# Seven half-size products for part of the first feed-forward matmul, with one set of keys and queries, in a sparse-attention and feed-forward kernel on one Trainium2 core

## The chip, the core and the metric

The kernel runs on one core of one Trainium2 chip. The core has five engines that run side by side and wait for each other through semaphores: TensorE (PE; its weight loads are listed as PEld), VectorE (DVE), ScalarE (ACT), GpSimd (POOL) and SyncE (SP). TensorE writes its results into PSUM, eight banks of 512 float32 per partition; VectorE and ScalarE read and write PSUM, GpSimd does not in this kernel. Each engine takes its instructions strictly in the order of its queue; transfers are issued from SP's queue and from GpSimd's. The metric is the device time of one execution, in microseconds (us). Three runs of the kernel before gave 212.04 us as their median, from 211.33 to 214.41.

## The reference

Four batches of eight heads, 768 positions, head size 64. Every query sees the keys fewer than 16 positions away, and one summary for each of 24 blocks of 32 keys (the maximum of the block's keys, with log 32 added to its score, and the mean of its values). The attention output of all heads, 3072 tokens by 512, goes through a feed-forward layer with a gelu in its sigmoid form:

```
mask_l = np.abs(pos[:, None] - pos[None, :]) < window          # window = 16
scores_s = scale * q @ k_sum.T + np.log(block)                 # k_sum: max over blocks of 32
a = softmax(concat([where(mask_l, scale * q @ k.T, -1e9), scores_s]))
x = a @ concat([v, v_sum])                                     # 3072 x 512 after joining the heads
h = x @ w_in                                                   # 512 x 2048
out = (h * sigmoid(1.702 * h)) @ w_out                         # 2048 x 512
```

Work on the chip is in 16-bit types with float32 accumulation.

## The kernel before

All work is written in one list of words, `ORDER`; each word calls one small function (the table `ops`, near the end, says which), and the list's order is the order of every engine's queue. A batch goes through these steps:

- **Loads and keys.** `lk`, `lq`, `lv` load keys, queries and values (GpSimd's queue, with a cast to bfloat16). Batch 1 is transposed on TensorE (`tk`, `tq`); batches 2 and 3 by transposing transfers on SP's queue (`xk` for keys, `xq` for queries). `xa` takes the block maxima of the keys for two pairs of heads (VectorE), `ka` copies the key halos, `kR` writes the maxima into the key tiles. `vm` sums the values by blocks on TensorE, `vb` finishes the sums, `sd` and `ha` copy block sums and value halos (SP). `gate` is a small copy on GpSimd that waits for such a copy, and so holds back the loads behind it.
- **Attention.** `s` scores, `e` exponential (ScalarE), `m` mask (VectorE), `v` weighted values, `nn` normalisation (VectorE), `t`/`c` or `d` the transposition of the result into `xT` (TensorE and a copy, or a transfer).
- **First feed-forward matmul (an "ff stage").** There are 16 tiles of 128 hidden units (nt), each for the left and the right half of the 768 tokens. The word `f.half.nt.k0123.bank` makes four matmuls of 384 columns, `g` the gelu of that half tile (ScalarE) into `gT`.
- **Second matmul (a "product stage").** Each batch is done in three steps t by Winograd's form of Strassen's scheme: seven products `p.t.1` to `p.t.7` of eight matmuls with 256 columns, where the plain form has eight. `gs` builds the four sums of gelu results it needs (VectorE, some on GpSimd), `ws` the four sums of the weights (once), `x` takes the products out of PSUM: products 1, 5 and 6 are copied to SBUF, 2, 3 and 7 are added to such a copy on VectorE, 4 is copied. `o` stores. The accumulators are `poA`, `poB`, `poC`.

While the products of one batch run, the attention of the next is put between them; so product stages carry scores, exponentials, masks and norms, and ff stages carry the loads, transposes and key maxima of the batch after. Batch 0 is started by a path of its own. In the text, ff 1 is the ff stage of batch 1, products 1 its product stage, and so on.

Two memory pools matter. Keys `kx`, queries `qT` and values `vw` exist twice; batches 0 and 2 use set 0, batches 1 and 3 set 1. Set 0 lies in the pool `even`. The function `seven_pool` closes that pool and can open another in its place; the list calls it as its last but two word (`P7.0`), where it opens nothing. The functions for seven products in the first matmul (`w_sum7`, `x_sum7`, `product7`, `taken7`, `gelu7`) are in the file, but the list calls none of them.

PSUM is six pools: banks 0 to 3 single, 4 and 5 double. `bank(42, ...)` and `bank(52, ...)` take a double bank, 40, 41, 50, 51 half of one. The ff tiles use 0 to 3.

Of the kernel before, what the change touches and what calls it, by code (L numbers as in the profile page):

```python
# [17 lines left out]
class _Ordered:  # L18


    def __init__(self, tc, eng):
        self._tc, self._eng = tc, eng

    def __getattr__(self, name):
        f = getattr(self._eng, name)

        def call(*a, **kw):
            r = f(*a, **kw)  # L28
            self._tc.keep_in_program_order(r)
            return r  # L30

        return call
# [11 lines left out]
f.0.2.k0123.1 s.0.1.3.42 e.1.3 f.0.1.k23 f.0.4.k0123.50 mf f.0.6.k0123.40 f.0.5.k0123.51 f.0.7.k0123.41 G f.0.3.k0123.0  # L44
g.0.2 g.0.0 g.0.1 g.0.4 g.0.6 g.0.3 lk.1.3 lq.1.0 g.0.7 g.0.5 lq.1.3 ck.1 m.1.0 m.1.2 ow.1 lk.1.4 lk.1.1 lk.1.2 lv.1.5.1
lk.1.5 lk.1.6 lq.1.2 lk.1.7 m.1.1 lq.1.1 lv.1.0.0 lq.1.4 lq.1.5 lq.1.7 lv.1.3.1 lq.1.6 lv.1.0.1 lv.1.2.0 lv.1.1.0 cv.1
lv.1.1.1 lv.1.4.0 lv.1.2.1 f.0.8.k0123.2 lv.1.4.1 late m.1.3 ws.0.0 g.0.8 f.0.9.k0123.3 f.0.11.k0123.0 g.0.9
f.0.10.k0123.1 v.0.1.0.40 v.0.1.1.41 lv.1.3.0 nn.1.0 g.0.11 g.0.10 v.0.1.2.50 f.0.13.k0123.3 f.0.12.k0123.2 t.1.0.42
v.0.1.3.51 nn.1.1 f.0.15.k0123.0 g.0.12 f.0.14.k0123.1 g.0.13 t.1.1.52 c.1.0.d c.1.1.d g.0.15 ws.0.1 g.0.14 f.1.8.k01.3
f.1.0.k01.2 f.1.8.k23 ha.1.3.0 f.1.9.k0123.0 f.1.0.k23 ws.1.1 g.1.8 g.1.9 f.1.1.k0123.1 ws.2.0 f.1.2.k0123.3 g.1.0  # L50
f.1.3.k0123.2 g.1.1 ws.1.0 gs.0.2.0 ha.1.2.0 f.1.10.k0123.1 g.1.3 gs.0.2.1 f.1.4.k0123.2 g.1.2 gs.2.2.2 g.1.10 lv.1.5.0
gs.0.2.3 f.1.11.k0123.1 g.1.4 f.1.12.k0123.3 g.1.11 f.1.13.k0123.0 ws.3.1 tk.0.52 g.1.13 gs.2.2.0 g.1.12 kc.0.a
f.1.6.k0123.2 gs.0.2.2 gs.2.2.1 f.1.15.k0123.0 f.1.5.k0123.1 ws.3.0 g.1.6 g.1.5 tk.1.52 kc.1.a tk.2.42 kh.0.1.d ws.2.1
f.1.14.k0123.3 f.1.7.k0123.1 tk.3.52 gs.2.2.3 kc.2.a xm.0.1 tq.0.42 gs.4.2.0 g.1.15 kc.3.d p.0.2.0 g.1.7 g.1.14 gs.6.1.0
p.0.1.2 qc.0.a xm.1.1 tq.1.52 ha.1.1.0 gs.4.2.2 lq.2.0 x.0.1.a gs.4.2.1 gs.6.1.2 lq.2.2 gs.6.1.1 gs.7.1.0 ha.1.0.0
qc.1.a gs.6.1.3 lv.2.0.0 tq.2.42 p.1.1.3 qc.2.a gs.7.1.1 gs.4.2.3 p.0.5.1 x.0.5.a p.0.6 tq.3.52 kr.0.1.d s.1.0.0.42
x.0.6.a x.0.2.a gs.7.1.2 X gs.7.1.3 kr.1.1.d x.1.1.d xm.3.1 kh.2.1.g p.1.2.0 e.0.0 p.0.3 p.0.7 lq.2.3 m.0.0 x.0.3.a
x.0.7.a kh.1.1.d qc.3.d s.1.1.0.42 e.1.0 p.1.6 xm.2.1 vm.1.42 o.0.0.0.0.2 s.1.0.1.52 lv.2.5.0 e.0.1 kr.2.1.g kh.3.1.d
p.0.4 vb sd.1.1.0 x.0.4.a gate.1 s.1.1.1.52 e.1.1 lv.2.3.0 p.1.5.1 kr.3.1.d x.1.5.d x.1.2.a m.1.0 x.1.6.a s.1.0.2.52
sd.1.0.0 p.2.1.2 m.0.1 x.2.1.a p.1.3 s.1.0.3.42 o.0.0.1.0.2 p.1.7 lv.2.1.1 e.0.2 m.1.1 lk.2.0 e.0.3 s.1.1.2.52 lk.2.2  # L60
lv.2.2.0 x.1.7.a x.1.3.a lv.2.2.1 lk.2.3 p.2.6 e.1.2 lv.2.5.1 s.1.1.3.42 m.0.2 p.1.4 v.1.0.0.50 e.1.3 v.1.0.1.51 lk.2.1
m.0.3 m.1.3 lk.2.4 v.1.1.0.40 v.1.1.1.41 x.2.6.a p.2.5.1 G lk.2.5 nn.0.0 nn.1.0 x.2.5.a lk.2.7 p.2.7 o.0.1.0.0.2
# [20 lines left out]
f.0.0.k23 lk.3.6 g.0.1 g.0.9 g.0.8 f.1.1.k0123.0 f.1.8.k0123.1 g.0.0 f.1.9.k0123.3 g.1.1 g.1.9 g.1.8 f.1.0.k0123.2
f.0.10.k0123.0 g.0.10 gate.2 g.1.0 gs.0.2.2 xk.1.1.0 f.1.2.k0123.1 gs.0.2.0.d gs.0.2.1 xk.1.0.1 f.1.10.k0123.3 g.1.2
o.1.1.1.0.2 g.1.10 lq.3.6 f.0.2.k0123.2 gs.0.2.3 lv.3.5.1 f.1.3.k0123.1 vm.3.52 g.1.3 xk.1.1.1 g.0.2 xk.1.0.0
o.1.2.1.0.2 f.0.13.k0123.0 f.0.3.k0123.2 f.1.11.k0123.3 f.0.12.k0123.1 g.0.3 g.0.13 g.1.11 xa.0.1 f.0.4.k0123.2 xq.1.1
f.1.12.k0123.3 lq.3.1 f.0.11.k0123.0 g.0.4 gs.2.2.2.g g.0.12 f.1.5.k0123.1 g.0.11 lq.3.2 vb xa.1.1 xq.1.0 f.0.5.k0123.2
# [12 lines left out]
f.1.13.k0123.3 g.1.2 f.1.3.k0123.1 g.0.10 f.0.3.k0123.2 g.1.13 f.1.10.k0123.3 g.0.3 f.0.11.k0123.0 f.0.4.k0123.2 g.1.3  # L100
# [13 lines left out]
def kernel(  # L114
# [849 lines left out]
```

## Time and profile before

| | before |
|---|---|
| median of three runs | 212.04 us |
| the profiled execution | 211.7 us, of it 210.0 us span from first to last instruction |
| granted TensorE clock | 0.996 |
| busy: TensorE / VectorE / ScalarE / GpSimd | 200.4 / 130.8 / 114.3 / 109.1 us |
| ff 1, ff 2, ff 3 | 77.21 to 99.32, 123.10 to 144.63, 167.10 to 187.90 us |
| products 0, 1, 2, 3 | 51.6 to 77.2, 99.3 to 123.1, 144.6 to 167.1, 187.9 to 206.4 us |

The profile is one execution, read by several views: the groups of instructions (line, engine, operation, tile written `<-` tiles read, shape, count | busy us and mean ns of one | idle time of the engine before them and what ended it); the timeline, which merges neighbours of one kind (start, length, engine, instruction, count, and in brackets the engine's idle time before); the chain that ended last; and the busy time in stretches. All lines stand under one source line, 28, since a helper issues every instruction, so the groups are told apart by their tiles: `ph` is the accumulator of the first matmul, `ps_s` of scores, `ps_av` of weighted values.

### The profile page before, as it was taken

The page shows a single profiled execution, that of the slowest core. Times are in us where ns is not written, and L with a number is a line of the kernel's source. Part 1 is how long each engine was busy: PE and PEld are TensorE (multiplying, and loading weights), DVE is VectorE, ACT ScalarE, POOL GpSimd, SP SyncE. Part 2 cuts the span into 40 slices and gives each one's busy share as a digit, 9 for nine tenths or more (in the row PEclk, how much of TensorE's full clock was granted, in tenths as well). Part 3 has the DMA queues.
Part 4 walks back from the last instruction along what each step waited for, and adds up shares of the span by engine and source line. Part 5 has one row for each costly group of instructions (what it writes and reads, how often), then busy time and mean ns, then how long its engine had stood idle before and what let it go on. Part 6 is the DMA issues. An engine that isn't in the chain of part 4 may idle for free.

```text
span 210.0 us, 5880 instructions
## 1 busy us (share of the span) xinstructions
PE 200.4 (95%) x2440; PEld 145.8 (69%) x2440; DVE 130.8 (62%) x311; ACT 114.3 (54%) x227; POOL 109.1 (52%) x157
## 2 busy tenths in 40 slices
PE   7998798999999999999999999999999999999993
PEld 5656554667887886556788865657888865668882
DVE  5577873798997871168997822694888500166342
ACT  2473885659666736676764336567670157671100
POOL 7999972399982998448949422431000000863000
PEclk9999999999999999999999999999999999999998
DMA  4999999999999999999999999939215920000214
GB/s 67 162 166 189 209 213 221 182 144 122 99 134 199 156 177 183 130 126 141 148 166 204 142 227 180 187 29 169 50 53 139 160 105 0 0 3 0 100 53 150
DMA packets 96458, 27.74 MB, mean 132 GB/s; under 512 B 85024, under 2 KB 93488, under 8 KB 96432
## 3 DMA queue, kind: packets, MB, share of 16 engines
q0 software_dynamic: 70800, 13.64, 82.7%
q1 hardware_dynamic: 25632, 13.74, 33.2%
q8 instruction: 19, 0.31, 0.6%
q14 instruction: 7, 0.06, 0.1%
HBM read 27.26 MB, written 6.29 MB: 160 GB/s over the span
## 4 chain that ended last, share of the span: by engine, by line
PE 79%; POOL 12%; DMA 5%; issue 1%; DVE 1%; SPq 0%; POOLq 0%; DVEq 0%
PE ph L28 36%; PE poA L28 19%; PE poB L28 10%; PE poC L28 5%; PE ps_s L28 3%; PE ps_av L28 3%; DMA vw<-vw 2%; POOL mk L28 2%; DMA out_dram<-osb 2%; POOL v0n L28 2%; POOL w_in_sb L28 2%; POOL kb L28 2%; POOL kx L28 2%; POOL qb L28 1%; PE ps_t L28 1%
## 5 line engine op out<-in xcount | busy, mean ns | idle before, releaser
L28 PE MATMUL ph<-xT,w_in_sb 128*128 128x384 f16 x512 | 86.1, 326 | 0.4 <-DVE osb L28 0.4
L28 ACT ACTIVATE gT<-ph 128x384 f16<-128x384 f32 x128 | 56.1, 495 | 30.6 <-PE ph L28 29.9
L28 PEld LDWEIGHTS <-w_in_sb 128*128 128x128 f16 x512 | 49.2, 98 | 32.4 <-issue 0.9
L28 PEld LDWEIGHTS <-gs 128*128 128x128 f16 x384 | 36.5, 98 | 4.6
L28 DVE TENSOR_TENSOR gs<-gT 128x768 f16<-128x768 f16 (+1 forms) x36 | 17.5, 498 | 29.1 <-ACT gT L28 29.0
L28 POOL TENSOR_TENSOR gs<-gs,gT 128x768 f16<-128x768 f16 (+1 forms) x6 | 8.8, 1461 | 41.8 <-PE ph L28 32.7
L28 POOL DMA_DIRECT2D kb<-in_k_dram x28 | 23.1, 842 | 13.7 <-DMA w_out_sb<-in_moe_w_out_dram 6.4
L28 ACT ACTIVATE a_sb<-ps_s 128x768 bf16<-128x768 f32 x32 | 24.8, 808 | 9.5 <-PE ps_s L28 9.3
L28 PEld LDWEIGHTS <-gT 128*128 128x128 f16 x288 | 27.3, 98 | 3.6
L28 POOL DMA_DIRECT2D vw<-in_v_dram x36 | 25.7, 752 | 5.0 <-DMA w_out_sb<-in_moe_w_out_dram 1.7
L28 PE MATMUL poA<-ws,gs 128*128 128x256 f16 x192 | 24.8, 273 | 0.0
L28 POOL DMA_DIRECT2D qb<-in_q_dram x28 | 23.8, 867 | 1.8 <-issue 0.9
L28 DVE TENSOR_TENSOR a_sb<-a_sb,mk 128x768 bf16<-128x768 bf16 x28 | 14.7, 550 | 3.0 <-ACT a_sb L28 2.2
L28 DVE TENSOR_TENSOR x<-ps_av,rc 128x768 f16<-128x768 f32 (+1 forms) x18 | 15.6, 869 | 0.6
L28 ACT ACTIVATE s<-poA 128x256 f32<-128x256 f32 x14 | 5.4, 382 | 19.3 <-PE poA L28 18.6
L28 PE MATMUL poB<-ws,gs 128*128 128x256 f16 x96 | 12.5, 273 | 0.0
L28 PE MATMUL poC<-w_out_sb,gT 128*128 128x256 f16 x96 | 12.5, 273 | 0.0
L28 PE MATMUL poA<-w_out_sb,gT 128*128 128x256 f16 x96 | 12.4, 273 | 0.0
L28 PE MATMUL poB<-w_out_sb,gs 128*128 128x256 f16 x96 | 12.4, 273 | 0.0
L28 PE MATMUL poA<-ws,gT 128*128 128x256 f16 x96 | 12.3, 273 | 0.0
L28 DVE TENSOR_REDUCE ka<-kx 128x48 bf16<-128x1536 bf16 x4 | 7.0, 1750 | 7.4 <-DMA kx<-kb 7.4
L28 ACT ACT_TABLE_LOAD x8 | 10.3, 1283 | 0.9 <-PEq L948 0.8
(102 smaller groups left out, 219.0 us busy)
## 6 DMA issues: line engine op xcount, KB each, us to landing
out_dram<-osb SPq DMA_DIRECT2D x23, 256.0 KB, 2.9
kb<-in_k_dram POOLq DMA_DIRECT2D x24, 96.0 KB, 6.0
qb<-in_q_dram POOLq DMA_DIRECT2D x24, 96.0 KB, 5.0
vw<-in_v_dram POOLq DMA_DIRECT2D x36, 64.0 KB, 5.1
w_out_sb<-in_moe_w_out_dram POOLq DMA_DIRECT2D x4, 512.0 KB, 14.8
w_in_sb<-in_moe_w_in_dram POOLq DMA_DIRECT2D x3, 512.0 KB, 11.3
vw<-vs SPq DMA_DIRECT2D x6, 198.0 KB, 3.9
kb<-in_k_dram POOLq DMA_DIRECT2D x4, 192.0 KB, 4.4
```

The source lines that it names most:

```text
L28: r = f(*a, **kw)
```

## The change

**The list.** In batches 1, 2 and 3 three, three and six of the eight pairs of ff tiles (j, j + 8) are made by seven products: pairs 2, 3, 4, again 2, 3, 4, and 2 to 7. The words `f` and `g` of these tiles go (48 half tiles), and for each pair come seven words `P.j.1` to `P.j.7` of two matmuls with 384 columns, four words `S` and three words `H`. Per batch four `U` build sums of `xT` (the token side), and eight words `W` in batches 0 to 2 build the sums of `w_in` for pairs 2 to 4 and 5 to 7, all on VectorE. The list after batch 0's first ff tiles is new throughout: batch 0's calls of the weighted values, the sums `ws` and `gs`, the loads, the transfers and the products stand in other places. GpSimd has as many `gs` words as before.

**A pair.** Products 1 and 5 open the two halves l and r of a double bank, "X". S1 copies l into a single bank "A" (ScalarE in batches 1 and 2, VectorE in batch 3), S5 copies r to SBUF as "h" (ScalarE). Product 2 is added to l; product 6 to A. S6 (VectorE) writes A + h into r; product 3 is added to r, product 7 to A. S7 (VectorE) adds A to h; product 4 is added to A. Then `H.j.0` makes the gelu of l and r at once (768 columns), `H.j.1` that of A, `H.j.2` that of h.

**One set of keys and queries.** `scores` reads set 1 for batches 1, 2 and 3, and `xk`, `xq` write it; values keep two sets. `P7.6.2`, called after batch 0's last scores, closes the pool with set 0 and opens the pool of the seven products in its place, for six pairs beginning at 2.

**Sums in place.** The third of the four `gs` sums is written over the right half of `gT` of tiles 0 to 7, of which nothing else is read; the `gs` tile is a quarter smaller.

**Program order.** The helper that issues instructions also records an edge, without a semaphore, from each instruction to the one before it on its engine.

```
-    vw = [sets[s].tile([128, NQ, H, VC], BF16, name=f"vw{s}") for s in range(2)]
+    vw = [keep.tile([128, NQ, H, VC], BF16, name=f"vw{s}") for s in range(2)]
...
-        score_tiles(st["S", half, p], p, b % 2, half)
+        score_tiles(st["S", half, p], p, min(b, 1), half)
...
+            1: (w_in_sb[:, 0:2, c], xTT[0][0], "l"),
+            2: (w_in_sb[:, 2:4, c], xTT[0][1], "l"),
+            6: (w[:, 1], x[:, 1], "A"),
+            5: (w[:, 0], x[:, 0], "r"),
+            7: (w[:, 2], x[:, 2], "A"),
+            3: (w[:, 3], xTT[1][1], "r"),
             4: (w_in_sb[:, 2:4, d], x[:, 3], "A")}[what]
+        if where is not None:
+            X = seven[j, "X"] = bank(where, F32, "phX")
+            seven[j, "l"], seven[j, "r"] = X[:, 0:HALF], X[:, 512:512 + HALF]
         for i in range(2):
+            pe.matmul(out=seven[j, name], lhsT=lhs[:, i], rhs=rhs[:, i], start=(what in (1, 5) and i == 0),
+                      stop=(i == 1), skip_group_check=True)
...
+    def taken7(j, what, eng, where=None):
+
+        if what == 1:
+            seven[j, "A"] = bank(where, F32, "phA")[:, 0:HALF]
+            copy(eng, seven[j, "A"], seven[j, "l"])
+        elif what == 5:
+            seven[j, "h"] = seven["pool"].tile([128, HALF], F32, name="r7", tag="r7", bufs=3)
+            copy(eng, seven[j, "h"], seven[j, "r"])
         else:
+            to = seven[j, "r"] if what == 6 else seven[j, "h"]
+            eng.tensor_tensor(out=to, in0=seven[j, "A"], in1=seven[j, "h"], op=ALU.add)
...
-        gs = snap.tile([128, 4, NT // 2, HALF], F16, name="gs")
+        t3 = snap.tile([128, 3, NT // 2, HALF], F16, name="gs")
+        gs = [t3[:, 0], t3[:, 1], gTb[:, 0:NT // 2, HALF:S], t3[:, 2]]
```

From the list, batch 0's attention values before and after:

```
-lv.1.1.1 lv.1.4.0 lv.1.2.1 f.0.8.k0123.2 lv.1.4.1 late m.1.3 ws.0.0 g.0.8 f.0.9.k0123.3 f.0.11.k0123.0 g.0.9
-f.0.10.k0123.1 v.0.1.0.40 v.0.1.1.41 lv.1.3.0 nn.1.0 g.0.11 g.0.10 v.0.1.2.50 f.0.13.k0123.3 f.0.12.k0123.2 t.1.0.42
+lv.1.2.0 lv.1.1.0 lv.1.1.1 lv.1.4.0 lv.1.2.1 f.0.8.k0123.2 lv.1.4.1 late m.1.3 f.0.9.k0123.3 f.0.10.k0123.1 v.0.1.0.40
+v.0.1.1.41 v.0.1.2.50 g.0.9 g.0.10 v.0.1.3.51 f.0.11.k0123.0 f.0.13.k0123.3 g.0.11 g.0.13 nn.1.0 t.1.0.42 f.0.14.k0123.1
```

and the end of ff 1 and of ff 2 after (a last letter d, a or g names VectorE, ScalarE or GpSimd; no letter, VectorE for `gs` and `xa`):

```
+f.1.14.k0123.2 H.2.2 g.1.14 f.1.15.k0123.3 lv.2.4.1 lq.2.5 P.4.2 P.4.6 P.3.4 S.4.6.d lq.2.7 g.1.15 f.1.13.k0123.3 H.3.0
+P.4.7 gs.6.1.0 xa.1.1 H.3.2 g.1.13 gs.0.2.1.g S.4.7.d lv.3.1.0 P.4.3 ka.1.g f.0.15.k0123.2 H.4.0 lk.3.0 f.1.7.k0123.3
+lk.3.4 vm.2.42 g.0.15 f.0.6.k0123.2 o.0.2.1.0.2 gs.2.2.0 H.4.2 P.4.4 g.1.7 g.0.6 f.0.7.k0123.3 kR.1.d lv.3.1.1 vb g.0.7
...
+H.2.1 S.4.1.a.0 P.3.7 P.3.3 xk.1.1.0 gate.2 S.4.5.a gs.6.1.0 xk.1.1.1 S.3.7.d o.1.1.1.0.2 lq.3.6 lv.3.5.1 xa.1.1
+f.0.14.k0123.3 P.4.6 g.0.6 H.2.2 H.3.0 f.1.7.k0123.2 P.4.2 g.0.14 g.1.7 P.3.4 lq.3.1 f.1.13.k0123.3 gs.6.1.1 S.4.6.d
+o.1.2.0.0.2 H.3.2 H.3.1 g.1.13 f.1.15.k0123.2 ha.3.3.0 gs.2.2.0 P.4.3 ha.3.0.0 H.4.0 ka.1.d P.4.7 g.1.15 kR.1.d vm.3.52
+xq.1.1 gs.6.1.3 S.4.7.d f.0.7.k0123.3 H.4.2 g.0.7 P.4.4 lq.3.2 p.0.1.2 ha.3.1.0 gs.2.2.1.g gs.7.1.0 gs.4.2.0 xq.1.0 vb
```

More of the change, by code (lines that the diff above doesn't have):

```diff
@@ L58 @@
[L58 to L62, printed above, removed]
@@ L83 @@
[L83 to L87, printed above, removed]
@@ L856, in taken @@
             name = {1: "s1", 6: "s2", 5: "s5"}[what]
-            p_ = seven.get("pool", snap) if what == 1 else snap
-            t_ = now[t, name] = p_.tile([128, N1], F32, name=name, tag=name)
+            t_ = now[t, name] = snap.tile([128, N1], F32, name=name, tag=name)
             copy(eng, t_, po)
```

182 lines of the change are left out of this document (84 added, 98 removed).

## The prediction

> **What bounds the kernel now.** I read the profile from its end: the chain that ended last, then TensorE's timeline, then the stages.
>
> ```profile
> span 210.0 us, 5880 instructions
> PE 200.4 (95%) x2440; PEld 145.8 (69%) x2440; DVE 130.8 (62%) x311; ACT 114.3 (54%) x227; POOL 109.1 (52%) x157
> ...
> L28 PE MATMUL ph<-xT,w_in_sb 128*128 128x384 f16 x512 | 86.1, 326 | 0.4 <-DVE osb L28 0.4
> ```
>
> In the chain, in order of time, hardly anything but TensorE stands from 34.69 us to 206.4 us; the four feed-forward stages are runs of `ph`:
>
> ```profile
> 29.38 5.17 DMA vw<-vw
> 34.55 0.14 issue
> 34.69 0.73 PE ps_av L28 x35
> ...
> 167.26 20.80 PE ph L28 x128
> ```
>
> So in the last batch a matmul of 384 columns costs 20.80/128 = 0.1625 us, back to back; the mean of 326 ns in the group is one matmul's passage through the array, overlapped with the next. The busy time by stage (columns: stretch, its length, then busy time and count of PE, PEld, DVE, ACT, POOL, the clock, DMA) has rows for ff 1, products 1, ff 2, products 2 and ff 3:
>
> ```profile
> 77.21:99.32 22.11, 22.11 (x190) 13.58 (x188) 10.86 (x17) 14.03 (x32) 14.89 (x20) 1.00 2.00 153
> 99.32:123.10 23.78, 22.93 (x362) 19.37 (x360) 19.79 (x47) 12.01 (x21) 14.83 (x20) 1.00 1.86 173
> 123.10:144.63 21.53, 21.53 (x176) 12.80 (x176) 12.40 (x25) 13.26 (x32) 6.70 (x7) 1.00 0.94 146
> 144.63:167.10 22.47, 22.47 (x361) 19.34 (x361) 17.07 (x39) 10.66 (x17) 0.91 (x1) 1.00 0.51 109
> 167.10:187.90 20.80, 20.80 (x130) 12.52 (x128) 3.56 (x5) 13.56 (x31) 8.32 (x5) 1.00 0.09 30
> ```
>
> TensorE is full in each ff stage, ScalarE about two thirds, VectorE half or less. A matmul less is time won, as long as the engines that pay for it keep behind TensorE. What is idle on TensorE after 34.69 us is small; the one wait inside that I use later is that ahead of ff 2:
>
> ```profile
> 123.10 8.61 PE L28 MATMUL ph<-xT,w_in_sb 128*128 128x384 f16 x52 [0.41 <-DVE osb L28]
> ```
>
> **The change part by part.** *Matmuls.* A pair of ff tiles (j and j+8, both halves) takes 4 x 4 = 16 matmuls of 384 columns; by seven products of two matmuls it takes 14. Twelve pairs (3+3+6) save 24, and the order's ff and P words do sum to 488 instead of 512. All stand on the chain: 24 x 0.1625 = **-3.9 us**.
>
> *What the pairs cost elsewhere.* The nearest rows:
>
> ```profile
> L28 ACT ACTIVATE gT<-ph 128x384 f16<-128x384 f32 x128 | 56.1, 495 | 30.6 <-PE ph L28 29.9
> L28 ACT ACTIVATE a_sb<-ps_s 128x768 bf16<-128x768 f32 x32 | 24.8, 808 | 9.5 <-PE ps_s L28 9.3
> L28 ACT ACTIVATE xT<-ps_x 128x384 f16<-128x384 f16 x3 | 1.4, 491 | 0.6 <-PE ps_x L28 0.6
> L28 DVE TENSOR_TENSOR x<-ps_av,rc 128x384 f16<-128x384 f32 x4 | 2.2, 558 | 0.1
> L28 DVE TENSOR_TENSOR osb<-poA,s 128x256 f32<-128x256 f32 x12 | 5.1, 422 | 3.7 <-PE poA L28 3.7
> L28 DVE TENSOR_TENSOR gs<-gT,gs 128x768 f16<-128x768 f16 x12 | 6.9, 589 | 0.1
> ```
>
> Per pair ScalarE gives four gelus (1.98 us) and takes one of 768 (0.81), two of 384 (0.99), S5 (0.49) and, in batches 1 and 2, S1 (0.49): +0.80 us, in batch 3 +0.31. VectorE takes S6 and S7 (0.56 each, between 0.42 for 256 columns and 0.96 for 768), in batch 3 S1 too; per batch four U (0.59 each), and eight W once. An engine that writes its result into PSUM is in no row; I take the 384-column reads of PSUM (0.49 and 0.56), with nothing and the 768-column 0.81 and 0.96 as ends. Summed over the queues by these rows, ff 1 has 20.0 us of matmuls from its third ff word on, 17.7 of ScalarE, 17.0 of VectorE; ff 2 20.4, 17.7, 16.3; ff 3 19.1, 17.1, 14.6. Back to back ScalarE is quicker than its mean:
>
> ```profile
> 169.58 2.12 ACT L28 ACTIVATE gT<-ph 128x384 f16<-128x384 f32 x5 [0.16 <-PE ph L28]
> ```
>
> Five start within 2.12 - 0.49, 0.41 us apart. So both keep up on average, and the added busy time costs nothing as load (in products 2 VectorE comes near its limit: the words there sum to 23.0 us for 18.8 before, so 17.07 becomes some 21.3 of 22.5; taken at 0, up to 1.0). It costs where TensorE, which takes its queue in order, stands before a result. A hand-over from TensorE takes about 0.2 us (the first gelu of ff 3 starts at 168.93, the tenth matmul after 167.10 is issued by 168.73), one to TensorE 0.05 (VectorE's last result before ff 2 ended at 122.63 + 0.42 = 123.05, the matmul began at 123.10):
>
> ```profile
> 167.10 20.96 PE L28 MATMUL ph<-xT,w_in_sb 128*128 128x384 f16 x128
> 168.93 0.49 ACT L28 ACTIVATE gT<-ph 128x384 f16<-128x384 f32 x1 [1.24 <-PE ph L28]
> 122.63 0.42 DVE L28 TENSOR_TENSOR osb<-poC,s 128x256 f32<-128x256 f32 x1 [1.16 <-DMA out_dram<-osb]
> ```
>
> *Batch 0.* The new order calls the attention values after two of the tiles 9, 10, 11, where the old one has three. They wait for the halo copies, which land at 34.55 whatever TensorE does. TensorE arrives 4 x 0.1625 earlier and waits so much longer: **+0.65** (0 if the copies come earlier, 0.9 with the old 0.28 us wait beside it).
>
> *Batch 1, the pinch.* On VectorE the key maxima `xa.0.1` stand ahead of S6 of pair 4, and `xa.1.1` ahead of its S7. In the old order only sums of gelus, not needed at once, stood behind them, and they did wait for key transposes:
>
> ```profile
> 67.04 0.18 POOL L28 COPY gate<-vw 32x1 bf16<-32x1 bf16 x1 [4.16 <-DMA vw<-vs]
> 78.41 8.40 SPq L28 DMA_TRANSPOSE kx<-kb  x4
> 90.75 1.75 DVE L28 TENSOR_REDUCE ka<-kx 128x48 bf16<-128x1536 bf16 x1 [5.92 <-DMA kx<-kb]
> 95.25 0.86 POOL L28 DMA_DIRECT2D kb<-in_k_dram  x1 [1.54 <-DMA kx<-kb]
> ```
>
> Counted from the first ff matmul (77.21) the pairs landed at +13.5 and +18.0. The loads that feed them start behind `gate.1`, itself behind batch 0's value sums; old order: 15.3 us from their end (61.93) to 77.21. New: eleven products of eight matmuls (0.875), six score tiles (0.28), four value tiles (0.22) and three transposes (0.33), 13.2 us. So all is 2.1 us later against ff: +15.6 and +20.1. Needed: P7 of pair 4 stands 19.5 us in (100 matmuls of 384 columns, two products, four value and two transpose groups), less 0.05, S6 0.56, a gs sum 0.59 and the maximum 1.75: +16.6. P4 stands at 22.7 (116 such matmuls and the sums' 0.53); less 0.05, 0.56, 1.75: +20.3. Both are met, by 1.0 and 0.2 us, with nothing over. I take **+0.7**, between 0 and 3.5 (landings later by the 1.5 to 4.5 us by which two transposes of this one stage differ).
>
> The single key set itself costs nothing: in both orders the transposes are called after the last scores of the batch before, which free the set.
>
> *Batch 2.* Here the transposes come early, but on VectorE stand between S7 of pair 3 and S7 of pair 4: `xa.1.1`, a gs sum, S6, `gs.2.2.0`, the key halos `ka.1.d` (three copies), the key rows and another gs sum; and GpSimd's `gs.2.2.1` starts as soon as `gs.2.2.0` is done. The old order had the same meeting in ff 2, with nothing urgent behind it:
>
> ```profile
> 138.75 0.53 DVE L28 COPY kx<-ka 128x576 bf16<-128x576 bf16 x2
> 139.66 2.10 DVE L28 COPY kx<-kx 128x320 bf16<-128x320 bf16 x3
> 139.84 1.71 POOL L28 TENSOR_TENSOR gs<-gs,gT 128x768 f16<-128x768 f16 x1 [3.12 <-DVE gs L28]
> 190.43 0.91 POOL L28 TENSOR_TENSOR gs<-gT,gs 128x384 f16<-128x384 f16 x1
> 190.72 0.42 DVE L28 TENSOR_TENSOR osb<-poC,s 128x256 f32<-128x256 f32 x1 [1.02 <-PE poC L28]
> ```
>
> The halo copies ended 0.21 us after GpSimd's sum did (141.76, 141.55): held by it; the last pair of rows shows a VectorE sum that reads PSUM beside a GpSimd sum at its usual 0.42, so S6 and S7 themselves aren't held. From the end of pair 3's P7: 0.2, S7 0.56, maximum 1.75, gs 0.3, S6 0.5, gs 0.5, halos 2.1, rows 0.5, gs 0.3, S7 0.56, 0.05: 7.3 us. Between the two products TensorE has 32 matmuls of 384 columns and the value sums, 5.2 + 0.53 = 5.7 us: it waits some 1.6 us, or 0.4 if the halos run free (about 0.9). I take **+1.3**, nearer the held case (0 to 2.0).
>
> The Trainium skill's page "SBUF — State Buffer", section "Who interferes with whom", says that a copy of VectorE in a two-port mode, or an instruction with two SBUF inputs against a GpSimd one that reads SBUF, blocks for the whole of the one that came first, while one SBUF input at most is free of it. The trace agrees (2.10 us with the 0.21 us behind GpSimd's end, and 0.42 unheld). It speaks against this change: the U, W and gs sums have two such inputs, and S7 waits in their queue. Were all twelve U held by 1.1 us (1.71 less 0.59), VectorE would lose 13 us; in this order GpSimd's sums meet them nowhere, so the sum has only the halos' case.
>
> The 0.41 us ahead of ff 2 goes, **-0.4**: it was the tile in the bank that VectorE's late result left; the new order starts with two other banks, 0.65 us ahead of that one. What is late next is ScalarE's copy of the last product's bank, 0.2 + 0.38 us, under the 0.875 us of another product.
>
> *Batch 3.* Six pairs run in twos on two double banks. Between P6 and P3, P7 and P4 mostly lie four to eight matmuls (0.65 to 1.3 us) against 0.2 + 0.56 + 0.05. In the last pairs P4 of pair 6 comes three matmul pairs after P7, and S6 of pair 6 stands late: some 0.3 us bare. On VectorE a gs sum that needs two of GpSimd's (1.65 to 1.75 us each) stands ahead of S1 of pair 7; these two start behind `gs.2.2.0` and end 0.35 us after the place where that S1 is wanted. **+0.7** (0 to 1.6).
>
> *The rest.* In-place gs[2], a smaller gs, vw out of the freed pool and the edges of program order add no instruction; taken at 0. The in-place sum puts a wait before the next batch's right-half gelus, until products 7 of the batch before; these lie a whole stage earlier.
>
> Sum: -3.9 + 0.65 + 0.7 + 1.3 - 0.4 + 0.7 = -0.95. The profiled execution had 211.7 us with its span of 210.0; less 0.95 its span would be 209.05. The median of the runs shown, 212.04, is 0.3 above the profiled execution, as near as these runs agree (211.33 to 214.41); I set the forecast against it: **211.1 us**.
>
> **The rivals.** *No new wait shows.* Then only -3.9 - 0.4 is left: 207.7 us. For it: TensorE's ff stages now have no wait inside. Against: the halo copies' landing doesn't depend on TensorE, and GpSimd's sum has met the key halos already.
>
> *The key transposes hold VectorE, slower than before.* In ff 1 TensorE waits for S6 and S7 of pair 4 behind the maxima. It begins to cost at landings past +16.6 and +20.3, and the kernel is slower than before from 0.95 + 0.7 = 1.65 us past these. For it: in ff 1 the transposes landed long after their issue (78.41 to 86.81 issued, 90.75 and 95.25 landed), with the loads beside them. Against: those loads come in the same number, so the margin is only what moved. Landing 4 us past: 211.1 - 0.7 + 4 = 214.4 us.
>
> *The hand-overs bind.* Each pair passes from TensorE to ScalarE or VectorE and back three times before its last gelu; were half a microsecond of it bare in each of twelve pairs, 6 us more: 217.1 us. It decides where fewer than 0.8 us of other matmuls lie between a product and its successor, which I find only at the ends of stages. ScalarE at 17.7 of 20.0 us speaks for it.
>
> *The change doesn't do what it says*: more than 488 ff matmuls, which the order's words exclude, or the added work not shorter than in the rows; 212 us and what that adds.
>
> **How the numbers follow.** Forecast 0.56, no new wait 0.13, late transposes 0.14, hand-overs 0.13, the rest 0.04. All low ends give -4.3 (207.7), all high ends -3.9 + 0.9 + 3.5 + 2.0 + 1.0 + 1.6 = +5.1 (217.1), but not together; the range 207.6 to 215.5 takes in the first, most of the second and the late transposes, and leaves out the hand-overs and a part of the rest, under 2 in 10. 2%, about what a measurement of this kernel can tell from no change, is 4.2 us: faster than 207.8 needs all of the matmuls and no wait, a half of that case, 0.07; slower than 216.3 needs the hand-overs or two of the high ends, 0.13; within, 0.80.
>
> **What would show it.** In the changed profile: 488 ff matmuls at 0.1625 us; a wait of nearly 1.9 us for the halo copies from 32.8 us; the maxima in ff 1 waiting for transposes, and TensorE behind VectorE there by about 0.7 us; one wait of about 1.3 us behind VectorE at the end of ff 2, with the key halos near 2 us beside a GpSimd sum; S6 and S7 near 0.56 us; less than a microsecond late in ff 3. Wrong would be: waits on TensorE of over 3 us in ff 1, many short waits behind ScalarE, or copies into PSUM far above 0.5 us.

## The result

The changed kernel is slower by about 1%: 213.67 us as the median of 20 runs against 212.18 us of the kernel before, a ratio of 1.0105 with a 95% interval from 1.0083 to 1.0128. Some runs of either kernel are in a slower state of the chip; all ratios here are of the other, fast runs alone, so they are not the quotients of the medians. The forecast was 211.1 us with a range of 207.6 to 215.5; the time lies inside the range, and on the other side of no change. The profiled execution took 214.25 us, of it a span of 212.4 us, 2.4 us more than before.

The head of the page and one of its groups, of the kernel after:

```profile
span 212.4 us, 5919 instructions
...
PE 197.3 (93%) x2416; PEld 141.8 (67%) x2416; DVE 156.6 (74%) x361; ACT 119.7 (56%) x233; POOL 108.6 (51%) x157
...
L28 PE MATMUL ph<-xT,w_in_sb 128*128 128x384 f16 x320 | 59.7, 326 | 0.7 <-DMA xT<-x 0.4
```

TensorE has 3.1 us less busy time (200.4 before) in a span that is 2.4 us longer: the work went, and idle time came. The view of waits for TensorE from 30 us on (engine, tile it was to write, what it waited for: us in total, how often, the longest), of the kernel after:

```profile
PE ps_av L28 <- DMA vw<-vw: 1.8, 2, 1.3
PE phA L28 <- DVE r L28: 0.9, 1, 0.9
PE poA L28 <- DVE gT L28: 0.6, 1, 0.6
PE poA L28 <- DVE s L28: 0.5, 1, 0.5
PE ph L28 <- DMA xT<-x: 0.4, 1, 0.4
PE poB L28 <- DVE gs L28: 0.3, 1, 0.3
PE poA L28 <- DVE gs L28: 0.3, 1, 0.3
PE phX L28 <- ACT r L28: 0.3, 1, 0.3
PE ph L28 <- ACT gT L28: 0.3, 1, 0.3
PE poB L28 <- DVE s L28: 0.2, 1, 0.2
```

The same view of before has four lines with 1.9 us in all, two of them VectorE's; here are ten with 5.6, and six end on VectorE. To add them up by stage I take the starts of neighbouring matmuls and subtract the usual step of their kind (0.1625 us for 384 columns, 0.109 for 256); a wait reads about 0.16 us longer in this way than as idle time, since the ends of matmuls are modelled. Losses over 0.18 us:

| stage | before | after | more | in the prediction's sum |
|---|---|---|---|---|
| batch 0, values | 1.38 | 2.13 | +0.75 | +0.65 |
| ff 1 | 0 | 0.71 | +0.71 | +0.7 |
| start of products 1 | 0.60 | 0.42 | -0.18 | 0 |
| ahead of ff 2 | 0.58 | 0 | -0.58 | -0.4 |
| ff 2, xT | 0 | 0.56 | +0.56 | 0 |
| ff 2, P.4.4 | 0 | 1.05 | +1.05 | +1.3 |
| products 2 | 0 | 0.87 | +0.87 | 0 |
| ff 3 | 0 | 0.94 | +0.94 | +0.7 |
| products 3 | 0 | 2.08 | +2.08 | 0 |
| sum | 2.56 | 8.76 | +6.20 | +2.95 |

Each column is one execution. With the 3.9 us of the matmuls that is +2.3, and the spans differ by 2.4. So what has to be explained is the 3.25 us between 2.95 and 6.20, and three places that the prediction had at zero make it (2.08 + 0.87 + 0.56): products 3, products 2 and the wait for xT.

Products 3 first. The timeline of the kernel after, in turn VectorE, GpSimd and TensorE (start, length, engine, instruction, count, idle time before it and what ended that):

```profile
189.15 1.79 DVE L28 TENSOR_TENSOR gs<-gT 128x384 f16<-128x384 f16 x1
...
191.66 0.34 DVE L28 TENSOR_TENSOR gs<-gT 128x384 f16<-128x384 f16 x1
...
192.20 0.41 DVE L28 TENSOR_TENSOR osb<-poC,s 128x256 f32<-128x256 f32 x1
192.53 0.73 DVE L28 TENSOR_TENSOR gs<-gs,gT 128x384 f16<-128x384 f16 x1
193.18 1.78 DVE L28 TENSOR_TENSOR gT<-gT 128x384 f16<-128x384 f16 x1
194.89 1.06 DVE L28 TENSOR_TENSOR gs<-gT,gs 128x384 f16<-128x384 f16 x1
```

```profile
188.84 1.88 POOL L28 TENSOR_TENSOR gs<-gs,gT 128x768 f16<-128x768 f16 x1 [1.09 <-DVE gs L28]
192.09 0.96 POOL L28 TENSOR_TENSOR gs<-gs,gT 128x384 f16<-128x384 f16 x1 [1.36 <-DVE gs L28]
193.01 1.75 POOL L28 TENSOR_TENSOR gT<-gT 128x768 f16<-128x768 f16 x1
194.72 1.02 POOL L28 TENSOR_TENSOR gs<-gT,gs 128x384 f16<-128x384 f16 x1
```

```profile
192.06 0.28 PE L28 MATMUL poB<-ws,gs 128*128 128x256 f16 x1 [0.33 <-DVE gs L28]
...
196.48 0.61 PE L28 MATMUL poA<-ws,gT 128*128 128x256 f16 x4 [0.59 <-DVE gT L28]
```

A VectorE sum of 384 columns takes 0.34 us at 191.66, where GpSimd stands idle. Four of the same size beside GpSimd's sums take 1.79, 0.73, 1.78 and 1.06, and each ends about 0.2 us after GpSimd's does (190.94 and 190.72, 193.26 and 193.05, 194.96 and 194.76, 195.95 and 195.74). That is 4.0 us on VectorE. TensorE's product waits inside its eight matmuls, for the last slice of the sum. The sum `osb<-poC,s` at 192.20, with one input in PSUM and one in SBUF, has its usual 0.41 beside GpSimd's sum of 192.09.

In the kernel before the same meeting was there, two sums of 0.55 in 2.26 us beside GpSimd's 1.76 (VectorE in the first view, GpSimd in the second):

```profile
185.79 2.26 DVE L28 TENSOR_TENSOR gs<-gs,gT 128x768 f16<-128x768 f16 x2
```

```profile
185.61 1.76 POOL L28 TENSOR_TENSOR gs<-gs,gT 128x768 f16<-128x768 f16 x1
```

It cost nothing, since TensorE had feed-forward tiles until 187.90 us. The new order has four such meetings later, at 188.8 to 195.7 us, when products 3 already run and each asks for the next sum.

The same thing at the end of ff 2 and in products 2, where the prediction had looked for one of the two:

```profile
141.20 2.10 DVE L28 COPY kx<-kx 128x320 bf16<-128x320 bf16 x3
...
143.93 0.55 DVE L28 TENSOR_TENSOR r<-phA,r 128x384 f32<-128x384 f32 x1
...
147.06 1.33 DVE L28 TENSOR_TENSOR gs<-gs,gT 128x768 f16<-128x768 f16 x1
```

```profile
141.36 1.72 POOL L28 TENSOR_TENSOR gs<-gs,gT 128x768 f16<-128x768 f16 x1 [11.03 <-DVE gs L28]
...
146.35 1.63 POOL L28 TENSOR_TENSOR gT<-gT 128x768 f16<-128x768 f16 x1
```

```profile
144.53 0.48 PE L28 MATMUL phA<-xs,w_in_sb 128*128 128x384 f16 x2 [0.89 <-DVE r L28]
...
148.91 1.03 PE L28 MATMUL poA<-ws,gs 128*128 128x256 f16 x8 [0.49 <-DVE s L28]
```

The key halos are held for GpSimd's sum, S7 of pair 4 (`r<-phA,r`) comes behind them, P.4.4 behind S7. Then a sum of 0.55 takes 1.33 beside GpSimd's next, and the copy `s<-poA` behind it lets TensorE wait once more (0.65 of the 0.87 by starts; the other 0.21 is a wait of scores at 147.09 for block sums that stand in VectorE's queue behind the halos).

### The profile page after: what moved, and what is told of

Its sections match the earlier page's. It is cut to its first block, busy times and chain, and to the rows that moved or that the text cites. A ratio compares the mean times of both kernels' runs of the same rounds, so it can differ in the third digit from the quotient of the medians.

```text
span 212.4 us, 5919 instructions
## 1 busy us (share of the span) xinstructions
PE 197.3 (93%) x2416; PEld 141.8 (67%) x2416; DVE 156.6 (74%) x361; ACT 119.7 (56%) x233; POOL 108.6 (51%) x157
## 5 line engine op out<-in xcount | busy, mean ns | idle before, releaser
L28 PE MATMUL ph<-xT,w_in_sb 128*128 128x384 f16 x320 | 59.7, 326 | 0.7 <-DMA xT<-x 0.4
L28 PEld LDWEIGHTS <-w_in_sb 128*128 128x128 f16 x392 | 37.5, 98 | 26.3 <-issue 3.5
L28 ACT ACTIVATE gT<-ph 128x384 f16<-128x384 f32 x80 | 36.7, 494 | 22.8 <-PE ph L28 22.3
L28 PEld LDWEIGHTS <-gT 128*128 128x128 f16 x384 | 36.4, 98 | 6.3 <-DVE gT L28 0.9
L28 PEld LDWEIGHTS <-gs 128*128 128x128 f16 x288 | 27.0, 98 | 6.6 <-DVE gs L28 2.1
L28 PE MATMUL poA<-ws,gT 128*128 128x256 f16 x192 | 24.8, 273 | 0.6 <-DVE gT L28 0.6
L28 PEld LDWEIGHTS <-ws 128*128 128x128 f16 x96 | 9.4, 98 | 6.8 <-issue 0.7
L28 PE MATMUL poA<-ws,gs 128*128 128x256 f16 x96 | 12.8, 273 | 0.9 <-DVE s L28 0.5
L28 DVE TENSOR_TENSOR gs<-gT 128x768 f16<-128x768 f16 (+1 forms) x19 | 11.0, 580 | 2.4 <-ACT gT L28 2.4
L28 DVE TENSOR_TENSOR phX<-phA,r 128x384 f32<-128x384 f32 x12 | 6.7, 562 | 7.7 <-PE phX L28 4.0
```

## The experiments

Two theories. **Held**: GpSimd's sums hold VectorE's, and TensorE waits for these. **Load**: VectorE has too much to do at the ends of the ff stages, 25.8 us more busy time in all (156.6 against 130.8; time in which a sum is held counts as busy), and would be late without GpSimd too. They differ in a sharp way: if GpSimd's sums are given to VectorE as well, the first says faster and the second slower. Ratios below are against the kernel before on the same chip. From the list only the words around an edit are shown.

### Four sums of batch 3 from GpSimd to VectorE

```
-x.0.2.a gs.0.2.1.g gs.7.1.1.g gs.6.1.1
-gs.0.2.3.d gs.0.2.2.g p.1.6 x.0.5.d p.0.7 gs.7.1.3.g
+x.0.2.a gs.0.2.1.d gs.7.1.1.d gs.6.1.1
+gs.0.2.3.d gs.0.2.2.d p.1.6 x.0.5.d p.0.7 gs.7.1.3.d
```

> The changed kernel with four gs sums of batch 3 (gs.0.2.1, gs.7.1.1, gs.0.2.2, gs.7.1.3) made by VectorE instead of GpSimd. Theory 'held': in products 3 VectorE's own sums stand behind GpSimd's (1.79, 0.73, 1.78 and 1.06 us for sums that take 0.34 alone, 4.0 us lost), and TensorE's waits there (0.33, 0.32, 0.59, 0.19) come from it. Without GpSimd beside them they take 0.34 each; VectorE gains 4.0 us and pays 1.8 us for the four sums (0.55, 0.34, 0.55, 0.34). TensorE's waits in products 3 fall from 1.4 us to under 0.5, and the time by 1.0 to 1.4 us, to about 212.5. Theory 'load': VectorE simply has too much to do at the end of ff 3 with S1, S6 and S7 of six pairs; four sums more make TensorE's waits 1 to 1.8 us longer, about 215.

Measured: 211.96 us, ratio 0.9989 [0.9953, 1.0024], against 1.0105 of the changed kernel. In the span's last 24 us the view of waits has no line for TensorE any more; by starts, 0.28 us is left of 2.08. The ratio falls by 1.2%, some 2.5 us, where 1.0 to 1.4 was expected and TensorE's waits make 1.8; the intervals allow that. VectorE with the sums of the timeline above:

```profile
189.06 0.35 DVE L28 TENSOR_TENSOR gs<-gT 128x384 f16<-128x384 f16 x1
...
191.26 1.09 DVE L28 TENSOR_TENSOR gs<-gs,gT 128x768 f16<-128x768 f16 x3
```

More work on VectorE, and its queue is done earlier: the last gs sum ends at 194.89 instead of 196.90. 'Load' falls for this stage.

### GpSimd's sums beside them, for nobody

The sums are VectorE's, as in the run before, and GpSimd makes sums of the same sizes whose result is read by no one:

```
+    def g_beside(j, n, what, eng):
+        k2 = slice(j + NT // 2, j + n + NT // 2)
+        eng.tensor_tensor(out=beside[:, 0:n], in0=gTb[:, k2, 0:HALF], in1=gTb[:, k2, HALF:S], op=ALU.add)
...
-x.0.2.a gs.0.2.1.d gs.7.1.1.d gs.6.1.1
-gs.0.2.3.d gs.0.2.2.d p.1.6 x.0.5.d p.0.7 gs.7.1.3.d
+x.0.2.a gd.0.2.1.g gs.0.2.1.d gd.7.1.1.g gs.7.1.1.d gs.6.1.1
+gs.0.2.3.d gd.0.2.2.g gs.0.2.2.d p.1.6 x.0.5.d p.0.7 gd.7.1.3.g gs.7.1.3.d
```

> The run in which VectorE makes the last four gs sums of batch 3 itself (211.96 us, 0.9989 of the kernel before), and beside them GpSimd makes four sums of the same sizes of other tiles, whose result nobody reads: VectorE and TensorE get no work and no wait for a result from it. Theory 'held': VectorE's sums beside them take up to 1.8 us again instead of 0.34 to 0.55, 2 to 4 us in all on top of 1.8 us more of its own work, and TensorE's waits in products 3 come back, 1.5 to 3 us: 213.5 to 215. If instead the gain came from results that GpSimd gave late (1.64 us for what VectorE does in 0.55), these sums cost nothing: 212.0.

Measured: 216.30 us, ratio 1.021 [1.017, 1.025]: 4.3 us more by the medians (on two chips) for instructions that nothing waits for. VectorE and GpSimd in the timeline:

```profile
187.40 1.56 DVE L28 TENSOR_TENSOR gs<-gT 128x768 f16<-128x768 f16 x1
...
191.07 1.78 DVE L28 TENSOR_TENSOR gT<-gT 128x384 f16<-128x384 f16 x1
```

```profile
189.95 3.68 POOL L28 TENSOR_TENSOR beside<-gT 128x384 f16<-128x384 f16 x3 [1.41 <-ACT gT L28]
```

The first of GpSimd's sums (186.89, 1.65 us) holds VectorE's at 187.40, which takes 1.56 instead of 0.55, and those from 189.95 on hold a sum of 0.34 for 1.78. VectorE is held again, by an engine that hands it no result and takes none from it. TensorE waits once for 2.6 us, and that wait has a second price, told at the end. The mechanism is shown: it is the two engines' meeting, not late results.

### Three sums at the end of ff 2 from GpSimd to VectorE

```
-P.4.4 lq.3.2 p.0.1.2 ha.3.1.0 gs.2.2.1.g gs.7.1.0 gs.4.2.0 xq.1.0 vb
-p.0.5.1 H.4.1 s.3.0.1.42 X s.3.0.2.52 gs.7.1.1.g gs.4.2.1 x.0.1.d
-p.1.1.3 x.0.6.d e.0.0 gs.2.2.2.g p.1.2.0
+P.4.4 lq.3.2 p.0.1.2 ha.3.1.0 gs.2.2.1.d gs.7.1.0 gs.4.2.0 xq.1.0 vb
+p.0.5.1 H.4.1 s.3.0.1.42 X s.3.0.2.52 gs.7.1.1.d gs.4.2.1 x.0.1.d
+p.1.1.3 x.0.6.d e.0.0 gs.2.2.2.d p.1.2.0
```

> The changed kernel with three gs sums around the end of ff 2 (gs.2.2.1, gs.7.1.1, gs.2.2.2) made by VectorE instead of GpSimd, at their places in the list. Theory 'held': the key halos (2.10 us beside GpSimd's 1.72) take about 0.9, S7 of pair 4 comes 1.2 us earlier, TensorE's wait of 0.89 us at P.4.4 goes, and so does most of the 0.49 us in products 2, since the VectorE sum of 1.33 us beside GpSimd's takes 0.55: 1.0 to 1.4 us less, about 212.5. Theory 'load': the maximum, S6, the halos and the sums are too long a queue in any case, the wait at P.4.4 stays over 0.5 us, and the 1.4 us of added sums make products 2 later: no gain, 213.7 to 214.5.

Measured: 212.30 us, ratio 1.0029 [0.9997, 1.0060]. The halos of this kernel, and S7 behind them:

```profile
141.18 0.66 DVE L28 COPY kx<-kx 128x320 bf16<-128x320 bf16 x3
...
142.46 0.55 DVE L28 TENSOR_TENSOR r<-phA,r 128x384 f32<-128x384 f32 x1
```

0.66 instead of 2.10, S7 1.47 us earlier, and no wait at P.4.4. In products 2 the waits that made 0.87 us are gone, and a new one of 0.44 us (by starts) stands at a later sum: the added 1.4 us of sums do cost a little, as 'load' said, but far less than the hold.

### Batch 0: two tiles ahead of the values

```
-f.0.10.k0123.1 v.0.1.0.40 v.0.1.1.41 v.0.1.2.50 g.0.9 g.0.10 v.0.1.3.51 f.0.11.k0123.0 f.0.13.k0123.3 g.0.11 g.0.13 nn.1.0 t.1.0.42
+f.0.10.k0123.1 f.0.11.k0123.0 g.0.9 f.0.13.k0123.3 v.0.1.0.40 v.0.1.1.41 v.0.1.2.50 g.0.10 v.0.1.3.51 g.0.11 g.0.13 nn.1.0 t.1.0.42
```

> The changed kernel with two tiles of batch 0's ff (f.0.11 and f.0.13) and the gelu g.0.9 called ahead of the weighted values v.0.1 instead of behind them. If the halo copies land at 35.0 us whatever TensorE does, TensorE's wait there falls from 1.8 us by 8 x 0.1625 = 1.3 us to 0.5, and the time to 212.4. Rival: what follows the values (normalisation, transposition, the loads behind the gate) waits for the same landing, and products 0 or ff 1 wait by so much more: 213.7, with new waits between 38 and 100 us.

Measured: 213.53 us, ratio 1.0079 [1.0041, 1.0117], not told apart from the changed kernel. TensorE's timeline:

```profile
34.88 0.92 PE L28 MATMUL ps_av<-vw,a_sb 128*64 128x65 bf16 x47 [0.54 <-DMA vw<-vw]
36.75 0.51 PE L28 MATMUL ps_x<-ident,x 128*128 128x128 f16 x6 [0.94 <-DVE x L28]
```

The wait for the halo copies, which land at 34.88 us (35.00 in the changed kernel), shrank to 0.54, and a new one of 0.94 us stands behind it: the transposition waits for VectorE's normalisation, which the two tiles had covered. The rival was right, with its wait nearer than it said.

### S7 ahead of the key maximum in ff 1

```
-P.4.7 gs.6.1.0 xa.1.1 H.3.2 g.1.13 gs.0.2.1.g S.4.7.d
+P.4.7 S.4.7.d gs.6.1.0 xa.1.1 H.3.2 g.1.13 gs.0.2.1.g
```

> The changed kernel with S7 of pair 4 in ff 1 called straight behind its product 7, ahead of a gs sum and of the key maxima xa.1.1 (1.74 us) on VectorE. If the maximum holds S7, and S7 the gelus behind it on ScalarE, S7 comes 1.4 us earlier and the 0.43 us that TensorE lost at 98.97 us behind a gelu goes: 213.2. If VectorE's queue is late as a whole there, the gs sums of products 1 come 0.3 to 0.5 us later instead and nothing is won: 213.7.

Measured: 213.94 us, ratio 1.0086 [1.0050, 1.0122]: nothing won. The wait behind the gelu is gone, and TensorE waits at the first scores of products 1 instead, for the block sums at the end of the same queue:

```profile
100.97 0.53 PE L28 MATMUL ps_s<-qT,kx 64*128 64x64 bf16 x24 [0.39 <-DVE vs L28]
```

VectorE's block sums are ready no earlier than in the changed kernel: they end at 100.87 us against 100.50, in an execution that is 0.36 us later at this place. So what is put ahead pushes something else behind. That VectorE has too much to do there is not shown by it: in this order it stands idle for 0.66 us ahead of S7, for product 7.

### Pairs as plain tiles

In three kernels, pairs were made by plain tiles at the places of the products: batch 3's, those of batches 1 and 2, and all. In them a tile of the right half stood at product 5 and read quarters of xT ahead of the words that call their transfer, so these read the batch before.

> The changed kernel with batch 3's six pairs as plain tiles (four matmuls of 384 columns each) at the places of the products, without batch 3's sums U and the sums W of pairs 5 to 7: 12 matmuls more, 1.95 us. Gone are the waits of ff 3 (0.28, 0.11, 0.26, 0.24 us) and VectorE's S1, S6 and S7 (18 of 0.56 us), so that its gs sums are ready earlier. If the pairs of batch 3 pay, it is slower than the changed kernel, up to 215; if what they cost in ff 3 and products 3 (0.9 and 2.1 us) outweighs the matmuls, 212.7, 1.0 us faster.

> The changed kernel with the three pairs each of batches 1 and 2 as plain tiles and without their sums U: 12 matmuls more, 1.95 us. Gone are the waits behind S7 and the late gelus: 0.28 and 0.43 in ff 1, 0.42 at the start of products 1, 0.89 at P.4.4, some of 0.88 in products 2, 2.0 to 2.9 us together: between 212.7 and 213.7. The wait of 0.40 us for xT and the 1.8 us for the halo copies stay.

> The changed kernel with all twelve pairs as plain tiles, without the sums U and W: 512 ff matmuls as in the kernel before, but the rest of the change (one set of keys and queries, the sums in place, the new order). From the kernel before differ then the values called one tile earlier (+0.65 us), the wait for xT (+0.40), no wait ahead of ff 2 (-0.4), and GpSimd's sums beside VectorE's in products 3 (0 if VectorE comes to them early, up to 1.4): 212.8 to 214.3.

Measured: 217.13 us, ratio 1.025 [1.0215, 1.0285]; 217.48 us, 1.028 [1.0235, 1.0326]; 221.77 us, 1.0443 [1.0391, 1.0496]. They tell little: in the first, TensorE waits 3.1 us for xT transfers, in the second 2.5, which the place of the tiles made. Two of the kernels were made anew with the quarters where the products had read them:

> The changed kernel with batch 3's six pairs as plain tiles, without batch 3's sums U and the sums W of pairs 5 to 7, this time with each quarter of a tile called only where the products of its pair had read the same part of xT (in the run before, 3.0 us of its 217.1 were waits for xT transfers, by the place where these tiles stood): 12 matmuls more, 1.95 us. If the pairs of batch 3 pay, it is slower than the changed kernel, up to 215.5; if their waits in ff 3 and products 3 (0.9 and 2.1 us) outweigh the matmuls, about 212.7. GpSimd's last four sums stay beside VectorE's in both cases, so by the theory 'held' most of the 2.1 us stays even without the pairs, and it is slower: 214.5 to 215.5.

> The changed kernel with the three pairs each of batches 1 and 2 as plain tiles and without their sums U, placed in the same manner: 12 matmuls more, 1.95 us. Gone are the waits behind S7 and the late gelus (0.28 and 0.43 in ff 1, 0.42 at the start of products 1, 0.89 at P.4.4, some of 0.88 in products 2), 2.0 to 2.9 us together, if the pairs cause them: 212.7 to 213.7. If the gelus and the loads are late by themselves, the waits stay and it takes 215.5.

Measured: 215.62 us, ratio 1.0127 [1.0078, 1.0177], and 216.81 us, 1.0212 [1.0157, 1.0266]. In the second, plain tiles make ScalarE late (3.6 us of waits for gelus), so whether its pairs cost as much as they win stays open. The ratio of the first is not told apart from the changed kernel's, so whether the pairs of batch 3 pay is not shown by the times either. What its trace shows is where the loss of products 3 comes from. The waits of TensorE in products 3 without any pair in batch 3:

```profile
PE poA L28 <- DVE gT L28: 0.6, 1, 0.6
PE poB L28 <- DVE gs L28: 0.4, 1, 0.4
PE poA L28 <- DVE gs L28: 0.3, 1, 0.3
PE poB L28 <- DVE s L28: 0.2, 1, 0.2
```

The same four lines as with the pairs, 2.16 us by starts. VectorE is rid of eighteen copies and sums of 0.56 us and stands idle for 7.9 us ahead of its gs sums; beside GpSimd's they take 1.79, 0.73, 1.78 and 1.06 us as before, and products 3 are as late. Their loss comes from where the order puts GpSimd's sums, not from the seven products.

### All four edits

Besides the three above (both moves of sums, batch 0), in ff 2 the tile f.0.8 changes places with f.1.1, which had waited for the last quarter of xT.

> The changed kernel with the edits of the three other runs of this call together, and in ff 2 the tile f.0.8 changes places with f.1.1, which waited 0.40 us for the last transposing transfer of xT. Theory 'held': the gains add, 1.2 + 1.2 + 1.3 + 0.4 = 4.1 us, to 209.6 us, about 1.2% under the kernel before. Theory 'load': only the edits of batch 0 and of xT count, 1.7 us, and VectorE's added sums cost 1 to 2.5 us: 213 to 214.5.

Measured: 210.01 us, ratio 0.9931 [0.9896, 0.9966]; faster than both kernels, by less than 1% and by nearly 2%. Batch 0's wait for the normalisation is there as in its own run. The profiled execution, the longest of the twelve (211.78 us), has one wait more that no other kernel shows: 1.2 us at 72.7 us, for batch 1's value halos. Then batch 0 was mended: f.0.14 and f.0.15 between the values and the transposition (g.0.8 and f.0.12 move with them).

```
+f.0.10.k0123.1 f.0.11.k0123.0 g.0.8 g.0.9 f.0.13.k0123.3 v.0.1.0.40 v.0.1.1.41 v.0.1.2.50 g.0.10 v.0.1.3.51 g.0.11 f.0.14.k0123.1
+f.0.15.k0123.2 g.0.13 nn.1.0 t.1.0.42 f.0.12.k0123.0 nn.1.1 g.0.14 c.1.0.d t.1.1.52 f.1.8.k01.3 g.0.15 g.0.12 c.1.1.d
```

> The run with all four edits (210.01 us, 0.9931), with batch 0 mended: f.0.14 and f.0.15 are called between the weighted values and the transposition t.1.0, where f.0.11 and f.0.13 stood. In the run of all four the transposition waited 0.94 us for VectorE's normalisation, with no tile left to cover it. If that wait ate the gain of the two tiles, 0.9 us comes back: 209.1, 0.989 of the kernel before. Rival: all that follows in batch 0 is set by the transfers and loads, and TensorE waits later by the same 0.9: 210.0.

Measured: 209.75 us, ratio 0.9880 [0.9832, 0.9927], with a span of 207.1 us in the profile. TensorE's waits from 30 us on are down to four:

```profile
PE ps_av L28 <- DMA vw<-vw: 0.5, 1, 0.5
PE phX L28 <- ACT r L28: 0.3, 1, 0.3
PE poB L28 <- DVE gs L28: 0.3, 1, 0.3
PE ph L28 <- ACT gT L28: 0.3, 1, 0.3
```

The difference between these last two versions is not clear of the noise (their intervals overlap, and they ran on two chips); that the wait of 0.94 us went is seen in the trace.

## Why the prediction was wrong

- **Matmuls, -3.9: right.** 320 plain ones and 168 in products make 488, with starts 0.1625 us apart.
- **Batch 0, +0.65: place right, size not shown.** It is +0.75 by starts between these two executions. But the list up to the values is the same in nine of the other profiled kernels (all but the three that edit batch 0), and their loss there is anything from 0 to 2.43 us; the median of the ten is 1.8, against 1.38 before. The halo copies do not land at a fixed time either, as the prediction took it: the values go on between 34.14 and 35.28 us in those ten, but for the two that had run at half clock at 19 to 29 us (35.3 and 36.4). What the prediction left out is that the cover of a tile can be wanted twice, ahead of the values and behind them.
- **ff 1, +0.7: the cause was wrong, and the size right by luck** (0.28 of the 0.71 is a hand-over at 90.10 us, elsewhere in the stage). It said that the maxima would wait for key transposes. They waited for nothing (7.0 us of work, no idle time ahead):

```profile
L28 DVE TENSOR_REDUCE ka<-kx 128x48 bf16<-128x1536 bf16 x4 | 7.0, 1742 | 0.0
```

  S7 did stand behind the maximum's own 1.74 us (from 95.78 on), and the gelu of S7's result held ScalarE's queue. TensorE then waited for a bank of a plain tile behind that gelu, 0.43 by starts, not at P.4.4:

```profile
97.44 0.54 DVE L28 TENSOR_TENSOR r<-phA,r 128x384 f32<-128x384 f32 x1
```

```profile
98.01 0.52 ACT L28 ACTIVATE gT<-r 128x384 f16<-128x384 f32 x1 [1.00 <-DVE r L28]
```

```profile
98.97 0.81 PE L28 MATMUL ph<-xT,w_in_sb 128*128 128x384 f16 x4 [0.27 <-ACT gT L28]
```

  The rival of late key transposes is out with it. S7 was late by GpSimd too. The gs sum ahead of that maximum took 1.11 us instead of 0.34, and ended 0.2 us after GpSimd's copies of the key halos:

```profile
94.02 1.62 POOL L28 COPY kx<-kx 128x320 bf16<-128x320 bf16 x3
```

```profile
94.74 1.11 DVE L28 TENSOR_TENSOR gs<-gT 128x384 f16<-128x384 f16 x1
```

  No run takes this meeting alone away, so what it costs TensorE stays open.
- **ff 2, +1.3: right**, place and mechanism, 1.05 by starts. The halos beside GpSimd took 2.10 as in the row of before; free they take 0.66, less than the 0.9 that the prediction assumed.
- **The 0.41 ahead of ff 2, -0.4: right**, but the first tiles of the right half then waited 0.56 for xT. In the new order four products, not five, stand between the last values of products 1 and ff 2: those values start at 118.38 us (117.27 before), their normalisation, behind a product's sum at 120.40, ends at 121.96 (120.73 before), the last transposing transfers are issued by 123.19 (122.49 before), and ff 2 starts at 122.76 (123.10 before). The prediction followed SP's queue for the keys and not for xT.
- **ff 3, +0.7: about right in size (0.94), not in place.** It put the loss at a gs sum ahead of S1 of pair 7 and at S6 of pair 6. The trace has 0.44 behind ScalarE's copy S5, and two hand-overs of 0.24 and 0.26 us.
- **Products 2 and 3, 0: wrong, and by the sums of the table this step decided the sign** (without their 2.95 us the waits grow by 3.25, less than the 3.9 of the matmuls). For products 2 the prediction had 0, up to 1.0 as load; for products 3 it had no term. The prediction quoted the right rule of the Trainium skill, page "SBUF — State Buffer", section "Who interferes with whom": a VectorE instruction with two SBUF inputs and a GpSimd one that reads SBUF wait for each other in full. It named the gs sums among those that have two. Then, behind a price worked out for the U sums, it said that "in this order GpSimd's sums meet them nowhere, so the sum has only the halos' case", and gave the gs sums no price. The quoted words hold for U and W (0.55 us each in the trace). For the gs sums they are wrong: from 188.8 us on GpSimd and VectorE build the last of them side by side, with 4.0 us lost on VectorE and 2.08 on TensorE, and in products 2 another 0.8 and 0.87. The trace agrees with the page's rule at each of these places (what VectorE has in hand ends 0.2 to 0.4 us behind GpSimd's sum); what failed was the walk through the order, which laid GpSimd's sums beside VectorE's at the end of ff 2 alone. The runs show it from both sides: without GpSimd's four sums the ratio is 0.9989, with four that nobody reads 1.021.
- **Copies into PSUM and S6, S7 at 0.49 and 0.56: right** (0.48 on ScalarE, 0.57 on VectorE; 0.56 for the sums).

That the time lies inside the range is no merit of the mechanism: the range reaches to both sides of no change.

Of the rivals, no new wait (207.7 us) is out. In the last version the waits by starts make 3.47 us against 2.56 before; with 3.9 us of matmuls less that would be 3.0 us, and the spans differ by 2.9. So the matmuls' price was there in full. The hand-overs that bind (217.1) are out: the short ones in ff 1 and ff 3 (0.28, 0.44, 0.24, 0.26) make 1.2 us of the 6.2.

## What to carry to other kernels

When work is given to VectorE or moved in time, list GpSimd's instructions with their starts and ends, and lay every VectorE sum of two SBUF tiles (and such copies as those of the key halos here) over them, to the end of the kernel: beside one it waits for what is left of GpSimd's, here up to 1.4 us for a sum of 0.34. Whether that matters is set by who waits next; the same meeting was free under feed-forward tiles and cost TensorE 2 us under products that use each sum at once. A sum that takes GpSimd 1.65 us and VectorE 0.55 is not a relief for VectorE, if both have to read at the same time.

## What was not expected of the hardware

The 2.6 us wait of the run with sums for nobody cost more than itself. The busy time by stretch (stretch, its length, busy time and count of PE, PEld, DVE, ACT, POOL, granted clock, DMA):

```profile
191.20:194.10 2.90, 0.28 (x1) 0.10 (x2) 2.90 (x4) 0.38 (x1) 2.35 (x2) 1.00 0.00 0
194.10:197.80 3.70, 3.70 (x19) 2.70 (x20) 3.02 (x9) 0.38 (x1) 0.00 (x0) 0.55 0.00 0
```

Right behind the wait the granted clock is 0.55, and matmuls start 0.21 us apart instead of 0.109 for about 3.4 us, some 1.6 us more; it explains why 4.3 us were lost where TensorE's waits grew by 3 (0.28 to 3.24 by starts). All six executions of this kernel had the same mean clock of 0.992. The Trainium skill's page "TensorE: Matmul & The Clock Gate", section "Part 1: The HAM clock gate", gives a window of about 3.4 us for both the fall after idle time and the return; the length of the slow stretch agrees with it, while a wait of 2.6 us already set it off here. It doesn't follow each such wait: in the first run with plain tiles in batches 1 and 2, TensorE waited 2.5 us ahead of 132.5 us and had the full clock (1.00) after it. Less idle time did it elsewhere: in the two runs with plain tiles in batches 1 and 2, TensorE waited 0.82 and 1.16, and 0.55 and 1.23 us, at the values of batch 0, and the eight matmuls of 384 columns behind took 2.35 and 2.46 us, where they took 1.47 behind waits of 0.53 and 1.27 in the changed kernel. So waits of TensorE that sum to 2 or 2.5 us can cost 1.6 us more, and their length alone does not tell whether they do.
